# Attention with decay and a mixture of experts: q, k and v of a chunk laid out as four separate arrays

## The chip, the core and the metric

The kernel runs on one core of a Trainium2 chip. Its engines are TensorE (PE in the profile, with its weight loads as PEld), VectorE (DVE), ScalarE (ACT), GpSimd (POOL) and SyncE (SP), which here issues nearly all plain transfers; 16 DMA engines move the data between HBM and the core's SBUF. The metric is the device time of one execution in microseconds, as the median of several runs.

## What is computed

The inputs are q, k and v of shape (4, 8, 768, 64) (batch, heads, positions, head size) and a mixture of 8 experts, all in float32. The reference, cut to its core:

```python
for t in range(S):                                   # retention: attention with a decay per head
    state = gamma * state + einsum('bhd,bhe->bhde', k[:, :, t], v[:, :, t])
    y[:, :, t] = scale * einsum('bhd,bhde->bhe', q[:, :, t], state)
x = y.transpose(0, 2, 1, 3).reshape(B * S, H * D)    # 3072 tokens of 512
logits = x @ w_gate                                  # 8 experts, the best one takes the token
for e in range(E):
    xe = x[expert_idx == e]
    out[expert_idx == e] = gate_w * (maximum(xe @ w1[e], 0) @ w2[e])
```

## The kernel before

The 3072 tokens are cut into 24 chunks of 128 positions (`NCH`), six for each batch. For each chunk there are four blocks of 128 rows (SBUF partitions) and 512 floats: q transposed, k transposed, v and k, index 0 to 3 in that order. The host lays them out in one array `qkv` of shape (24, 128, 4, 512), so that one row of a chunk, all four blocks of it, is 8 KB in one piece in HBM.

The loop over chunks works on pairs, n = 0 to 11. For each chunk there are scores from q and k (`scores`, line 256, then a causal mask on DVE, line 259), the state's update from scaled v and k (`scale`, line 240, mostly on POOL, and `update`, line 271), the output from the scores and from the carried state (`output`, line 303, and `carry`, line 290), transposes to token rows (`rows`, line 322) and the gate's logits (`logits`, line 351, copied to LT by ACT at line 354, and turned back by PE as lp at line 363). The gating gives each token its expert and slot, and POOL scatters the token rows by indirect DMA (line 753) into `x_sorted` in HBM, where each expert has a region.

While that goes on, four loads of 1 MiB bring the weights of expert 0 (`fetch`, line 130, into tiles called raw: 128 rows of four pieces of 512 floats), and ACT and POOL or DVE split them into a high and a low part (lines 138 and 139).

The order on every engine is written out by hand; there is no planner. All of SP's transfers go through its one queue, in the order in which they are issued. `load(g)` (line 227) brings chunk g. Chunks 0 to 4 are brought as two halves, blocks 0 and 1 and then blocks 2 and 3 (512 KiB each), the other 19 whole (1 MiB). Four buffers of the pool `ld` and eleven of the pool `w` hold the chunks, so that SP issues the loads of chunks 0 to 14 at the start with no wait for a buffer, and those of chunks 15 to 23 as buffers come free. Two of the weight loads stand behind chunks 7 and 10 in the queue, the other two among the later chunks.

The last load, chunk 23, is followed on SP's queue by `start_rows` (line 453), which writes padding rows from the constants `cs` behind the rows of expert 0 in `x_sorted`, and by `fetch_early`, which waits for these rows and for the scatters of the first 18 chunks and brings the first 320 rows of expert 0 (line 148, tile xg). In the last pair, `turn_early` transposes them on DVE (line 768, xt), ACT casts them to the high part (line 775, xh), and PE uses xh in `early_pieces` (line 808, ph), the first work of the experts, which fills PE while the last gating is done. After that come the remaining rows of expert 0 and the other seven experts, ordered by their number of tokens, with two products each in three terms of high and low parts.

Of the kernel before, what the change touches and what calls it, by code (L numbers as in the profile page):

```python
# [18 lines left out]
E, DM, F = 8, 512, 1024  # L19
N = B * S  # L20
P = 128
# [3 lines left out]
NCH = B * CPB  # L25
# [75 lines left out]
def retention_moe(ctx, tc, qkv, w1, w2, cst, gdec, out):  # L101
    nc = tc.nc
# [101 lines left out]
    with ExitStack() as actx:  # L204
# [12 lines left out]
        qs, vss, Sbs, xTs, lgs, Ys, xrows = {}, {}, {}, {}, {}, {}, {}  # L217
# [4 lines left out]
        def load(g, part=slice(0, 4)):  # L222
            if g not in qs:
                early = AHEAD <= g < FIRST or g in MID
                qs[g] = (wp.tile([P, 4, DM], F32, name="qkv_w", tag="w", bufs=11) if early else
                         ld.tile([P, 4, DM], F32, name="qkv_t", tag="ld"))
            nc.sync.dma_start(out=qs[g][:, part], in_=qkv[g][:, part])

        def turned(g, i):
            return qs[g][:, i].rearrange("a (p t) -> a p t", p=NP)  # L230
# [259 lines left out]
        halves = (slice(0, 2), slice(2, 4))  # L490
        nc.vector.memset(wgs, 0.0)
        load(0, halves[0])
        gs = buf[0:2, 4 * NP * C:4 * NP * C + P + NP * C]
        nc.scalar.dma_start(out=gs, in_=gdec)
        nc.scalar.dma_start(out=cs[:, 0:NFIRST], in_=cst[:, 0:NFIRST])
        load(0, halves[1])
        for part in halves:
            load(1, part)
# [233 lines left out]
    natural = {0: (sidxs[0], metas[0]), E1: (sidxs[E1], metas[E1])}  # L732
# [484 lines left out]
```

## Time and profile before

| | |
|---|---|
| median of 3 runs | 395.36 us (394.53 to 395.36) |
| the profiled execution | 395.4 us |
| its span, first to last instruction | 393.5 us |
| PE busy | 385.6 us, 98% of the span |
| granted TensorE clock | 0.998 of full speed |
| DMA packets | 42332, 81.53 MB, 207 GB/s over the span |

The span leaves out what lies around the program's instructions, here 1.9 us. All stretches below are counted in microseconds from the span's start. PE's busy time says that it had an instruction in hand, not that it ran at its peak. In a stretch, the DMA share is the time that packets started in it took, over the time of 16 engines; it can pass 1.00, for the packets of one engine overlap somewhat.

### The profile page before, as it was taken

Reading aid. Unit: us, or ns where it says so; the run is one execution under the profiler, and the core shown is the slowest. Engines: PE = TensorE matmul, PEld = TensorE weight load, DVE = VectorE, ACT = ScalarE, POOL = GpSimd, SP = SyncE. Lnnn points to the kernel's source line nnn. Section 1 sums busy time; section 2 is a strip of 40 time slices with the busy share of each in tenths; the row PEclk is TensorE's granted clock in tenths of the full one; section 3 lists DMA queues with packets and bytes.
Section 4 is the critical chain, followed back from the end, with each engine's and each line's share of the span. In section 5 each row is a group of like instructions: output and inputs, shape, how many; then the busy total and the mean of one; then the engine's idle time right before and its main releaser. Section 6 shows DMA issues by size and latency. Waiting matters only on the chain.

```text
span 393.5 us, 8303 instructions
## 1 busy us (share of the span) xinstructions
PE 385.6 (98%) x3275; PEld 359.1 (91%) x3275; DVE 242.1 (62%) x467; ACT 141.3 (36%) x248; POOL 184.5 (47%) x175
## 2 busy tenths in 40 slices
PE   8999999999999899999999999999999999999994
PEld 4888888888999789999999999999999999999984
DVE  2567658966635796773874577386737658675310
ACT  2224344353311553532442354054335416423200
POOL 1656877784250427100682077038407813840743
PEclk9999999999999999999999999999999999999999
DMA  7999999983149759637472665564554636430111
GB/s 270 420 420 421 414 423 421 419 326 70 53 181 229 271 189 295 217 104 195 142 246 57 160 234 172 99 217 149 181 144 161 234 82 236 154 129 0 48 55 48
DMA packets 42332, 81.53 MB, mean 207 GB/s; under 512 B 4460, under 2 KB 18160, under 8 KB 39860
## 3 DMA queue, kind: packets, MB, share of 16 engines
q1 hardware_dynamic: 36768, 67.46, 50.7%
q0 software_dynamic: 5376, 13.49, 9.2%
q8 instruction: 26, 0.43, 0.4%
q14 instruction: 14, 0.11, 0.1%
q10 hardware_dynamic: 148, 0.04, 0.0%
HBM read 65.90 MB, written 15.68 MB: 207 GB/s over the span
## 4 chain that ended last, share of the span: by engine, by line
PE 94%; DVE 3%; issue 1%; ACT 1%; POOL 0%; POOLq 0%; DVEq 0%; ACTq 0%
PE ph L1050 31%; PE py L1078 27%; PE sp L256 5%; PE Y L303 5%; PE ph L808 4%; PE acc L827 4%; PE py L1076 3%; PE tr L322 3%; PE Y L290 3%; PE U L271 2%; PE L L351 2%; PE py L907 1%; PE py L968 1%; PE warm L507 1%; PE hn L951 1%
## 5 line engine op out<-in xcount | busy, mean ns | idle before, releaser
L753 POOL DMA_INDIRECT out<-Z,sidx x90 | 103.3, 1147 | 139.8 <-DVE Z L934 114.5
L139 DVE TENSOR_TENSOR wlo<-raw,whi 128x1024 fp32r<-128x1024 f32 (+1 forms) x57 | 68.4, 1205 | 14.3 <-ACT whi L138 13.9
L138 ACT CAST whi<-raw 128x1024 fp32r<-128x1024 f32 (+1 forms) x72 | 67.0, 950 | 8.2 <-DMA raw<-w 8.2
L1078 PE MATMUL py<-hh,whi 128*128 128x452 f32 (+5 forms) x192 | 66.9, 349 | 0.0
L1078 PE MATMUL py<-hl,whi 128*128 128x452 f32 (+5 forms) x192 | 66.9, 348 | 0.0
L1078 PE MATMUL py<-hh,wlo 128*128 128x452 f32 (+5 forms) x192 | 66.8, 348 | 0.0
L1055 ACT ACTIVATE hh<-ph 128x452 fp32r<-128x452 f32 (+6 forms) x56 | 28.3, 507 | 81.6 <-PE ph L1050 81.6
L1056 DVE SCALAR_TENSOR_TENSOR hl<-ph,hh 128x452 fp32r<-128x452 f32 (+6 forms) x56 | 32.1, 574 | 29.5 <-ACT hh L1055 29.0
L1050 PE MATMUL ph<-xh,wlo 128*128 128x452 f32 (+6 forms) x224 | 50.1, 345 | 0.0
L1050 PE MATMUL ph<-xh,whi 128*128 128x452 f32 (+6 forms) x224 | 50.1, 345 | 0.0
L1050 PE MATMUL ph<-xl,whi 128*128 128x452 f32 (+6 forms) x224 | 50.0, 345 | 0.0
L1050 PEld LDWEIGHTS ph<-xh,whi 128*128 128x128 f32 x224 | 40.8, 188 | 0.9
L1050 PEld LDWEIGHTS ph<-xh,wlo 128*128 128x128 f32 x224 | 40.8, 188 | 0.8
L1050 PEld LDWEIGHTS ph<-xl,whi 128*128 128x128 f32 x224 | 40.7, 188 | 0.7
L1078 PEld LDWEIGHTS py<-hl,whi 128*128 128x128 f32 x192 | 36.0, 188 | 0.8
L1078 PEld LDWEIGHTS py<-hh,wlo 128*128 128x128 f32 x192 | 36.1, 188 | 0.7
L1078 PEld LDWEIGHTS py<-hh,whi 128*128 128x128 f32 x192 | 36.1, 188 | 0.7
L775 ACT CAST xh<-buf 128x512 fp32r<-128x512 f32 (+7 forms) x26 | 14.3, 555 | 58.1 <-DVE buf L768 58.1
L259 DVE TENSOR_TENSOR Sb<-sp,cs 128x512 f32<-128x512 f32 x48 | 29.9, 681 | 2.7 <-PE sp L256 2.6
L753 POOL DMA_INDIRECT x_sorted<-xrow,KEY x24 | 24.2, 1008 | 15.1 <-DVE lp L391 7.3
L929 DVE STREAM_TRANSPOSE Z<-py 128x416 f32<-128x416 f32 (+3 forms) x24 | 15.0, 627 | 24.5 <-PE py L1078 24.4
L782 DVE TENSOR_TENSOR xl<-buf,xh 128x512 fp32r<-128x512 f32 (+7 forms) x26 | 18.1, 695 | 15.8 <-ACT xh L775 15.8
(172 smaller groups left out, 543.3 us busy)
## 6 DMA issues: line engine op xcount, KB each, us to landing
raw<-w SPq DMA_DIRECT2D x32, 1024.0 KB, 5.2
qkv_w<-qkv SPq DMA_DIRECT2D x12, 1024.0 KB, 18.5
qkv_t<-qkv SPq DMA_DIRECT2D x7, 1024.0 KB, 15.6
qkv_t<-qkv SPq DMA_DIRECT2D x8, 512.0 KB, 6.2
buf<-x_sorted SPq DMA_DIRECT2D x12, 211.2 KB, 3.7
x_sorted<-cs SPq DMA_DIRECT2D x6, 260.0 KB, 6.8
buf<-x_sorted SPq DMA_DIRECT2D x8, 195.0 KB, 3.6
out<-Z,sidx POOLq DMA_INDIRECT x90
```

The costliest lines, as they stand in the source:

```text
L138: nc.scalar.copy(out=hi[:, h], in_=raw[:, h])
L139: engine.tensor_tensor(out=lo[:, h], in0=raw[:, h], in1=hi[:, h].bitcast(F32), op=ALU.subtract)
L256: nc.tensor.matmul(out=sps[r][:, p, :], lhsT=kt[half[r], p, :], rhs=q[half[r], p, :], start=True, stop=True)
L259: nc.vector.tensor_tensor(out=Sb[:, r], in0=sps[r], in1=causal.unsqueeze(1).broadcast_to([P, NP, C]), op=ALU.mult)
L303: nc.tensor.matmul(out=at(Y, g, half[o], r, m), lhsT=vp[:, p, half[r]], rhs=Sb[:, r, p, :], start=False, stop=True, skip_group_check=True)
L753: sc = tc.nc.gpsimd.indirect_dma_start(out=dst, out_offset=bass.IndirectOffsetOnAxis(ap=index, axis=0), in_=rows, in_offset=None, bounds_c ...
L782: engine.tensor_tensor(out=xl[:, :, sl], in0=xt[:, :, t0:t0 + w], in1=xh[:, :, sl].bitcast(F32), op=ALU.subtract)
L808: nc.tensor.matmul(out=phs[f], lhsT=a[:, n % KD, fo:fo + P], rhs=h[:, n % KD, :], start=(n == 0), stop=(n == 11))
L1050: nc.tensor.matmul(out=ph[:, :cap], lhsT=wparts[e, f // 4][a][:, kd, fo:fo + P], rhs=x[:, kd, :cap], start=(n == 0), stop=(n == 3 * KD - 1))
L1055: nc.scalar.activation(out=hh[:, :cap], in_=ph[:, :cap], func=AF.Relu)
L1056: nc.vector.scalar_tensor_tensor(out=hl[:, :cap], in0=ph[:, :cap], scalar=0.0, in1=hh[:, :cap].bitcast(F32), op0=ALU.max, op1=ALU.subtract)
L1078: nc.tensor.matmul(out=py[:, :cap], lhsT=a[:, f % 4, k * P:(k + 1) * P], rhs=x[:, :cap], **se)
```

## The change

The host lays out the four blocks of a chunk one behind the other: `qkv` has the shape (24, 4, 128, 512), and a row of one block, 512 floats or 2 KB, is the longest piece that lies together for one partition. The load names the same elements in the same order of partitions, so the tiles in SBUF and all that reads them are as before; only the source's access pattern is another.

```diff
-            nc.sync.dma_start(out=qs[g][:, part], in_=qkv[g][:, part])
+            nc.sync.dma_start(out=qs[g][:, part], in_=qkv[g, part].rearrange("i p d -> p i d"))
...
-        "qkv": np.stack([transposed(q), transposed(k), natural(v), natural(k)], axis=3).reshape(NCH, P, 4, DM),
+        "qkv": np.stack([transposed(q), transposed(k), natural(v), natural(k)], axis=2).reshape(NCH, 4, P, DM),
```

A whole chunk was 128 pieces of 8 KB and is 512 pieces of 2 KB; a half was 128 pieces of 4 KB and is 256 of 2 KB. The host's layout is no part of the time.

## Rows read from the trace of the kernel before

**Rows 1.** The page: PE's busy time, and the DMA rate in 40 slices

```profile
PE 385.6 (98%) x3275; PEld 359.1 (91%) x3275; DVE 242.1 (62%) x467; ACT 141.3 (36%) x248; POOL 184.5 (47%) x175
...
GB/s 270 420 420 421 414 423 421 419 326 70 53 181 229 271 189 295 217 104 195 142 246 57 160 234 172 99 217 149 181 144 161 234 82 236 154 129 0 48 55 48
```

**Rows 2.** Windows: length, each engine's busy time and instructions, clock, DMA share, GB/s

```profile
97.00:128.00 31.00, 31.00 (x233) 30.11 (x230) 16.55 (x71) 7.39 (x20) 9.30 (x10) 1.00 0.53 149
128.00:393.00 265.00, 259.33 (x1400) 250.04 (x1398) 162.48 (x244) 97.92 (x142) 113.02 (x97) 1.00 0.50 157
```

**Rows 3.** DMA issues of the chunks: count, size of each, median us to landing

```profile
qkv_w<-qkv SPq DMA_DIRECT2D x12, 1024.0 KB, 18.5
qkv_t<-qkv SPq DMA_DIRECT2D x7, 1024.0 KB, 15.6
qkv_t<-qkv SPq DMA_DIRECT2D x8, 512.0 KB, 6.2
...
qkv_w<-qkv SPq DMA_DIRECT2D x2, 512.0 KB, 10.8
```

**Rows 4.** Windows, columns as in rows 2: stretches of 8, 2, 2, 4, 2 KB

```profile
57.00:62.00 5.00, 5.00 (x112) 4.44 (x112) 3.92 (x13) 1.35 (x5) 0.88 (x2) 1.00 1.02 429
24.00:26.00 2.00, 2.00 (x34) 1.36 (x25) 1.64 (x3) 0.81 (x2) 0.76 (x1) 1.00 1.09 428
34.00:36.00 2.00, 2.00 (x47) 1.81 (x43) 0.95 (x7) 0.24 (x1) 1.81 (x2) 1.00 1.02 393
...
10.00:13.00 3.00, 3.00 (x66) 2.66 (x64) 1.24 (x3) 0.37 (x1) 1.79 (x2) 1.00 1.03 422
126.00:132.00 6.00, 6.00 (x33) 5.22 (x32) 3.25 (x8) 3.27 (x5) 3.51 (x3) 1.00 1.05 407
```

**Rows 5.** DMA queues, packets, MB, share of 16 engines: 57:61, then 34.5:35.7 us

```profile
q1 hardware_dynamic: 231, 1.70, 100.7%
...
q1 hardware_dynamic: 214, 0.47, 102.4%
```

**Rows 6.** Timeline of SP's queue, 64 to 92 us: start, length, issue

```profile
64.44 6.82 SPq L227 DMA_DIRECT2D qkv_t<-qkv  x3
83.48 0.36 SPq L453 DMA_DIRECT2D x_sorted<-cs  x1
89.37 1.85 SPq L148 DMA_DIRECT2D xg<-x_sorted  x4
```

**Rows 7.** Landing of chunk 23 (issued 70.22), of start_rows; SP's wait for scatters

```profile
DMA to landing us min/median/max: 15.9/15.9/15.9
...
DMA to landing us min/median/max: 5.4/5.4/5.4
...
SPq L148 <- DMA x_sorted<-xrow,KEY: 5.4, 1, 5.4
```

**Rows 8.** Timeline, 94 to 98 us: the fetched rows on DVE, ACT and PE

```profile
94.73 1.63 DVE L768 STREAM_TRANSPOSE xt<-xg 128x512 f32<-128x512 f32 x3 [0.72 <-DMA xg<-x_sorted]
...
95.48 1.52 ACT L775 CAST xh<-xt 128x512 fp32r<-128x512 f32 x3 [0.98 <-DVE xt L768]
...
97.06 0.59 PEld L808 LDWEIGHTS ph<-xh,whi 128*128 128x128 f32 x4 [0.17 <-ACT xh L775]
```

**Rows 9.** Timelines near 19 and 39 us; landing of the weight load of 19.0

```profile
18.76 1.04 POOL L240 TENSOR_TENSOR vs<-qkv_w,cs 128x512 f32<-128x512 f32 x1 [1.92 <-DMA qkv_w<-qkv]
...
20.61 0.60 PEld L271 LDWEIGHTS U<-vs,qkv_w 128*64 128x64 f32 x16
...
DMA to landing us min/median/max: 19.4/19.4/19.4
...
38.12 1.14 ACT L138 CAST whi<-raw 128x512 fp32r<-128x512 f32 x2
39.89 0.37 ACT L354 COPY LT<-L 128x256 f32<-128x256 f32 x1 [0.64 <-PE L L351]
...
40.53 0.25 PEld L363 LDWEIGHTS lp<-cs,LT 128*128 128x128 f32 x2
```

## The prediction

> **What bounds the kernel now.** I read the page first: PE is counted busy for 98% of the span, and the DMA rate stands at 414 to 423 GB/s in the slices from 10 to 79 us, then falls [rows 1]. So there are two limits side by side in the first quarter (attention, which reads q, k and v): PE on its work, and the DMA engines on theirs. The windows by stage then show that behind 97 us PE has next to no idle time: 31.00 of 31 us, and 259.33 of 265 us, of which the rest is the tail after its last matmul [rows 2]. What makes PE late at 97 us is therefore paid in full at the end, and the question is only whether the loads make it late there or earlier.
>
> **What the change does to a load.** Nothing is computed differently and no instruction is added: 29 load issues on SP stay 29, of 19 x 1 MiB and 10 x 512 KiB [rows 3]. A whole chunk now comes in packets of 2 KB in place of 8 KB, so 512 packets in place of 128; a half chunk (two of the four arrays, so 4 KB in a row before) also comes in packets of 2 KB, 256 in place of 128. SP's cost of an issue I leave at nothing: its issues are hidden under a queue that is many microseconds deep (chunk 23 lands 15.9 us after its issue [rows 7]); without that cover it would be some tenths each.
>
> **The price of a smaller packet.** The trace has packets of all three sizes, because the weight loads (raw, 512 floats in a row) already come in 2 KB. With 8 KB packets alone the engines move 429 GB/s (57 to 62 us), with 4 KB packets 422 (10 to 13 us). Stretches that are mostly 2 KB packets give 393 (34 to 36 us) and 428 (24 to 26 us), both short, with packets of 8 KB at their edges, which are counted at their start; the one long stretch without 8 KB packets, 126 to 132 us, of 2 KB packets and some slightly larger writes, gives 407 [rows 4]. A second reading is free of these edges: bytes over the time that the packets themselves took. From 57 to 61 us that is 1.70 MB in 1.007 x 16 x 4 = 64.4 engine-us, 26.4 GB/s an engine; from 34.5 to 35.7 us it is 0.47 MB in 1.024 x 16 x 1.2 = 19.7 engine-us, 23.9 GB/s [rows 5]. That is 10% less, and an upper bound, for packets of one engine overlap somewhat (shares over 100%), and 2 KB ones can overlap more.
>
> I take 400 GB/s for 2 KB packets, between 393 and 407, and 429 and 422 for 8 KB and 4 KB. The 19 whole chunks are 19.92 MB: 49.8 us in place of 46.4, +3.4 us. The ten halves are 5.24 MB: 13.1 in place of 12.4, +0.7 us. Rounded, the sum is **+4.0 us** of DMA time up to the last chunk. Lower bound, at 407: (48.9 - 46.4) + (12.9 - 12.4) = +3.0; below that only if the 428 of 24 to 26 us is the true rate, which makes nothing of it. Upper bound, at 10% for whole chunks and half of that for halves: 4.6 + 0.6 = +5.2.
>
> The Trainium skill, "DMA: Bandwidth & Descriptors", section "Why small descriptors are slow (HBM only)", gives a fixed cost of some 3 cycles for each packet, beside one cycle for 32 bytes. By an estimate from that, four packets of 64 + 3 cycles stand against one of 256 + 3, 3.5% more (2.3% for halves): 46.4 x 0.035 + 12.4 x 0.023 = +1.9 us instead of +4.0. The rows ask for about twice that, and I go by the rows.
>
> **Whether the lateness adds up.** A late load is only passed on if the engines have no idle time in which to catch up. They have none from about 10 to 79 us: the slices hold one rate [rows 1], and the windows in them have packets in flight for over 100% of the time [rows 4]. The queue always holds several loads, because SP issues them as buffers come free, far ahead: 18.5 us is the median to landing of the 12 whole ones in the wide pool [rows 3]. So each chunk is late by the sum of all before it: some 0.8 us at chunk 4 or 5, about 1.8 us at the second weight load, nearly 4 us at chunk 23.
>
> **Where PE first feels it.** Early, at three near misses:
> - Chunk 4: POOL's scale waited 1.92 us for it and ended at 19.80; PE's update needs it at 20.61 [rows 9]. With 0.7 us (four chunks in halves and this one, 0.07 a half) it ends at 20.5: still in time.
> - The second weight load, issued at 19.0, lands after 19.4 us, at 38.4; the second of the two casts at 38.12 needs it, and behind them on ACT stands the copy of LT at 39.89, which PE waits for at 40.53 [rows 9]. Late by five chunks in halves (0.7) and six whole ones (1.0), so 1.7 us, it pushes the cast to 40.2 to 40.8 and LT's end to about 41.3: PE loses some 0.7 us here.
> - Later chunks have more room than they lose; PE, being 0.7 us later itself, gains as much room.
>
> These are no part of the sum, for PE's next meeting with the loads takes them in:
>
> **Where it is paid.** Behind load 23 on SP's queue stands the fill of padding rows in x_sorted (start_rows, issued at 83.48), and behind that the fetch of the first sorted rows (fetch_early). Chunk 23 was issued at 70.2 and landed 15.9 later, at 86.1; the fill landed after 5.4, at 88.9 [rows 6, 7]. SP waited 5.4 us from 83.84 for the last scatter of rows, to 89.24, and issued the fetch at 89.37 [rows 6, 7]. So the fill is only 0.4 us behind the gate. The rows fetched reached DVE's transposes at 94.73 (DVE had waited 0.72 us for them), ACT's casts to xh end at 95.48 + 1.52 = 97.00, and PE's first matmul on xh is at 97.06, after 0.17 us of waiting for ACT [rows 8]. That chain is tight from end to end. With chunk 23 late by 4.0, the fill goes behind it and lands at 92.9, the fetch leaves at 93.0, xh ends at 100.6, and PE, which would have been there at 97.8 after its early loss, waits for it. PE's loss at this point: 4.0 - 0.4 = **+3.6 us**, in place of the early 0.7 and not on top of it. The scatters that form the old gate share the engines with the loads; with 2 KB packets opposite theirs they get a larger share and do not become later than the fill.
>
> Behind 97 us PE has no idle time that could shrink [rows 2], and every later fetch depends on what PE and DVE compute, so it all moves together. The profiled execution took 395.4 us (span 393.5), the same as the median of the three runs, 395.36. **Forecast: 395.4 + 3.6 = 399.0 us.**
>
> **The rivals.**
> - *No cost at all*: 2 KB packets run at the rate of 8 KB ones, as the 428 of 24 to 26 us has it [rows 4], and the change does only what it says to the layout. Then chunk 23 lands at 86.1 as before and the time is 395.4, or 395.2 if the row scatters, which alternate with smaller packets, land up to 0.4 us earlier, down to the fill's landing. It decides as long as the lateness at chunk 23 stays under 0.4 us. Against it: 393 and 407 in the other two stretches. The Trainium skill, same page, "Rules for kernel authors", asks for 128 partitions and 1 MiB per DMA for full bandwidth and names no packet size; by that rule, which the whole chunks meet before and after, this rival is what happens. 0.13.
> - *Half the cost*: the mean of the two short stretches, 410 GB/s, is right. Then 19.92 MB take 48.6 us (+2.1) and the halves 12.8 (+0.4), 2.5 late, 2.1 paid: 397.5. For it: those stretches are the ones in this stage. The estimate from the skill's page above ends near here, at 395.4 + 1.9 - 0.4 = 396.9. 0.14.
> - *More than the sum*: packet time counts in full, 5.2 us late, 4.8 paid, 400.2; chunk 5 and chunk 15 then also reach PE's score matmuls late. Against it: the engines overlapped packets in every stretch. 0.07.
> - *Faster*: it would need a stretch in which four 2 KB reads beat one of 8 KB by more than 0.2%; no row shows one. What the smaller packets let through sooner (the scatters) frees at most the 0.4 us above. 0.04.
>
> **How the numbers follow.** The forecast has 0.62, about 398.0 to 399.9 (lateness of 3.0 to 4.9). Under 0.2% (0.8 us), about what a measurement of this kernel can tell from no change, lie the rival without cost and a little of the half-cost one. Slower: 0.62 + 0.14 + 0.07 - 0.01 = 0.82; same 0.14; faster 0.04. The range would leave out more than 2 in 10 if it stopped above the no-cost rival (0.13 + 0.04 below, and some 0.05 above 400.3), so it goes down to 395.3, which takes in the larger part of that rival, and up to 400.3, which takes in most of the high case.
>
> **What would show it.** In the new profile: packets under 8 KB nearly all; 395 to 405 GB/s in the slices from 10 to 80 us in place of 420; the stretch at that rate lasting some 4 us longer; chunk 23's landing near 90 and the fill's near 93; the fetch of xg near 93; PE's wait for xh before its first ph matmul grown from 0.17 to about 3 us, and a wait before lp near 41 us for LT. Behind that, each stage as long as before. I am wrong if the rate stays at 420 (no cost), if the rate falls but SP's fill and fetch do not move (the engines caught up somewhere), or if PE's total of waits before 90 us grows by more than the one at xh.

## The result, and the profile after

The kernel after the change takes 397.4 us (median of 20 runs, 395.43 to 399.95), the one before 394.7 in the same comparison (20 runs, 394.44 to 395.46). The ratio is 1.0069, interval 1.0049 to 1.0089: slower by 0.7%. The forecast was 399.0, in a range from 395.3 to 400.3. The profiled execution took 399.18 us, with a span of 397.4 us beside 393.5 before, so it is 3.9 us longer.

The 20 runs lie in two groups, ten from 395.4 to 396.8 and ten from 398.0 to 400.0. The mean granted clock is 0.996 to 0.999 in the lower group and 0.992 to 0.996 in the upper. No run took the median of 397.4, which is halfway between the groups. The profiled execution belongs to the upper one. No profile of the lower group was taken.

**The load rate.** From the page of the kernel after, PE's busy time and the DMA rate in 40 slices (against [rows 1]):

```profile
PE 386.7 (97%) x3275; PEld 359.8 (91%) x3275; DVE 241.8 (61%) x467; ACT 141.3 (36%) x248; POOL 184.6 (46%) x175
...
GB/s 298 400 405 405 406 408 407 407 358 74 0 189 166 361 115 302 223 167 173 155 179 94 193 167 231 71 197 191 161 169 137 247 76 225 168 133 0 48 54 48
```

The slices from 10 to 79 us stand at 400 to 408 GB/s in place of 414 to 423, and the ninth holds 358 in place of 326, because more is left to move. PE's busy time grew by only 1.1 us: the rest of the 3.9 us is idle time. PE's waits from 5 to 110 us are those of the kernel before (two of 0.2 and 0.3 us) and one more:

```profile
PE ph L808 <- ACT xh L775: 2.8, 1, 2.8
```

Windows of the kernel after, in the columns of [rows 2]; the first two are stretches of [rows 4], and the last two are what lies behind the first matmul on xh:

```profile
10.00:13.00 3.00, 3.00 (x62) 2.83 (x60) 1.24 (x3) 0.37 (x1) 2.58 (x3) 1.00 1.04 395
...
57.00:62.00 5.00, 5.00 (x108) 4.03 (x103) 4.05 (x11) 1.29 (x5) 1.22 (x2) 1.00 1.06 410
99.45:130.45 31.00, 31.00 (x220) 29.64 (x221) 14.96 (x68) 7.35 (x20) 8.29 (x9) 0.94 0.48 129
130.45:397.00 266.55, 260.80 (x1410) 251.48 (x1408) 163.36 (x246) 97.80 (x142) 114.05 (x98) 1.00 0.50 158
```

Pure chunk loads now run at 410 GB/s where they ran at 429 (57 to 62 us; E2 and E1 below have 405 and 428). Behind the first ph PE is again busy without a gap, 31.00 of 31 us, yet it gets through 220 matmuls in place of 233, at a mean clock of 0.94. Finer windows of the kernel after show where:

```profile
99.45:100.40 0.95, 0.95 (x6) 0.95 (x7) 0.95 (x3) 0.92 (x2) 0.41 (x1) 1.00 0.00 0
100.41:103.82 3.41, 3.41 (x20) 2.25 (x19) 2.23 (x13) 1.17 (x3) 0.00 (x0) 0.50 0.00 0
```

For 3.41 us TensorE is granted 0.50, that is 1.2 GHz in place of 2.4. Ahead of ph PE had stood idle for 2.8 us.

**The gate** is what SP waits for before it issues the fetch of the first sorted rows. The timeline of SP's queue after, 62 to 96 us, and SP's longest wait in that stretch (against [rows 6, 7]):

```profile
63.94 11.19 SPq L227 DMA_DIRECT2D qkv_t<-qkv  x3
82.76 0.38 SPq L453 DMA_DIRECT2D x_sorted<-cs  x1
90.77 1.85 SPq L148 DMA_DIRECT2D xg<-x_sorted  x4
```

```profile
SPq L148 <- DMA x_sorted<-cs: 7.5, 1, 7.5
```

What SP waits for ahead of the fetch is now the fill (x_sorted<-cs); before it was the last scatter of rows. By the semaphore records chunk 23 lands at 89.87 (86.09 before) and the fill at 90.63 (88.86 before). The last scatter, which was the gate before at 89.24, lands at 89.23. The fetch leaves at 90.77, 1.40 later than before.

SP's issues of the loads, which the prediction left at nothing, grew too: the three in the first line take 11.19 us in place of 6.82 with the waits between them [rows 6], that of chunk 23 alone 5.37 us in place of 1.04. At the gate this held nothing up: the fill was issued at 82.76, sooner than before.

The fetched rows on DVE, ACT and PE, from the timelines of the kernel after (against [rows 8]):

```profile
97.14 1.63 DVE L768 STREAM_TRANSPOSE xt<-xg 128x512 f32<-128x512 f32 x3 [3.63 <-DMA xg<-x_sorted]
...
97.89 1.52 ACT L775 CAST xh<-xt 128x512 fp32r<-128x512 f32 x3 [3.90 <-DVE xt L768]
...
99.45 0.59 PEld L808 LDWEIGHTS ph<-xh,whi 128*128 128x128 f32 x4 [3.06 <-ACT xh L775]
```

PE begins ph at 99.45, 2.39 us later than before. From there to the end of the span are 297.95 us, in place of 296.44: another 1.5, which the stretch at half clock explains. 2.4 + 1.5 = 3.9. The chain of work that ended last, in order of time (start, length, what), shows the path from the fetch to ph:

```profile
69.28 16.81 DMA qkv_t<-qkv
...
87.27 3.71 POOL wlo L139 x3
...
92.17 4.89 DMA xg<-x_sorted
...
97.14 0.72 DVE xt L768
...
97.89 1.52 ACT xh L775 x3
...
99.45 1.20 PE ph L808 x6
```

Its first two lines are not the path: the view puts the fetch down to the third of POOL's splits (wlo), which ended at 90.97, while the fetch's first issue was under way. In the kernel before the same split ended at 89.95, behind that issue (89.37 to 89.71), so the fetch does not wait for it. What ended SP's wait is the fill.

A piece of the path is the last quarter of the fetch: 4.89 us from its issue at 92.17 to its landing at 97.06. Before, the last quarter took 3.89, from 90.76 to 94.65. The DMA rate from 90.8 to 97.2 us, in 40 slices of 0.16 us, shows the last part of it as a trickle of a few packets, no slice above 16 GB/s from 95.3 us on:

```profile
GB/s 0 0 0 0 0 3 101 98 120 286 302 244 299 296 244 221 185 150 176 176 192 208 208 304 156 111 68 42 16 0 6 10 10 10 6 16 0 0 0 0
```

**Early.** The copy of LT near 39 us is not late, and PE's loads for lp follow at 40.02 without a wait (against [rows 9]; timelines of ACT and PEld after):

```profile
38.48 0.62 ACT L138 CAST whi<-raw 128x512 fp32r<-128x512 f32 x1 [0.25 <-issue]
39.38 0.38 ACT L354 COPY LT<-L 128x256 f32<-128x256 f32 x1 [0.29 <-PE L L351]
```

```profile
40.02 0.25 PEld L363 LDWEIGHTS lp<-cs,LT 128*128 128x128 f32 x2
```

### The profile page after: what moved, and what is told of

The parts are those of the page before. It is cut to its first block, busy times and chain, and to the rows that moved or that the text cites. A ratio compares the mean times of both kernels' runs of the same rounds, so it can differ in the third digit from the quotient of the medians.

```text
span 397.4 us, 8303 instructions
## 1 busy us (share of the span) xinstructions
PE 386.7 (97%) x3275; PEld 359.8 (91%) x3275; DVE 241.8 (61%) x467; ACT 141.3 (36%) x248; POOL 184.6 (46%) x175
## 4 chain that ended last, share of the span: by engine, by line
PE 88%; DMA 5%; DVE 1%; POOL 1%; ACT 1%; issue 1%; SPq 0%; POOLq 0%; DVEq 0%; ACTq 0%
PE ph L1050 31%; PE py L1078 27%; DMA qkv_t<-qkv 4%; PE sp L256 4%; PE ph L808 4%; PE acc L827 4%; PE Y L303 3%; PE py L1076 3%; PE tr L322 2%; PE Y L290 2%; PE U L271 2%; PE py L907 1%; PE py L968 1%; PE L L351 1%; DMA xg<-x_sorted 1%
## 5 line engine op out<-in xcount | busy, mean ns | idle before, releaser
L929 DVE STREAM_TRANSPOSE Z<-py 128x416 f32<-128x416 f32 (+3 forms) x24 | 15.0, 626 | 24.9 <-PE py L1078 24.9
## 6 DMA issues: line engine op xcount, KB each, us to landing
qkv_w<-qkv SPq DMA_DIRECT2D x12, 1024.0 KB, 13.2
qkv_t<-qkv SPq DMA_DIRECT2D x7, 1024.0 KB, 13.4
```

## The experiments

The theory: smaller packets make the loads later; the lateness is paid at one place, where PE waits for xh; and the idle time there costs some clock besides. The rivals: that the cost is in the queue order on SP (the fill behind load 23), that it comes once with any packet under 8 KB, or that it is spread over many small waits. E1 to E4 were timed beside a kernel before at 395.23 us (median of 14 runs, 394.46 to 395.56). In E5 to E12 the kernel before itself took 404 to 413 us (two single runs of 765 and 1486 us apart), so those are compared with that alone, and their traces with each other.

**E1, the kernel before once more** (no edit).

> The kernel before, unchanged, for a second trace. If the landings belong to the kernel: chunk 23 lands at 86.1 +- 0.5 us, the fill of x_sorted at 88.9, PE waits under 0.5 us for xh, the clock holds its upper level behind 97 us. PE's first score matmul and the clock's rise (6.3 us in the first trace, 4.8 in the changed kernel's) may lie anywhere between 4.8 and 6.3: if they are early here, the changed kernel's start, 0.6 us earlier, is no gain of the change. Rival: they are at 6.3 again, and the smaller first packets bring that gain.

It took 395.39 us. Chunk 23 landed at 86.55, the fetch left at 89.60, ph began at 97.14 after 0.17 us of waiting, and no stretch at half clock followed. PE's first weight loads on xh:

```profile
97.14 0.59 PEld L808 LDWEIGHTS ph<-xh,whi 128*128 128x128 f32 x4 [0.17 <-ACT xh L775]
```

So the two traces of the kernel before agree.

**E2, the kernel after once more** (no edit).

> The changed kernel, unchanged. Theory: DMA at 400 to 410 GB/s from 5 to 85 us, chunk 23 at 89.5 to 90, the fill at about 90.6, PE waits 2 to 3 us for xh; where a stretch of half clock follows that wait the run takes about 399, where none does about 396 to 397. Rival: the two groups of times come from the loads themselves (chunk 23 at 86 to 87 in the fast ones).

398.57 us (395.45 to 399.16), ratio 1.007, interval 1.0046 to 1.0094. Its timeline of PE's weight loads, and the window behind:

```profile
99.33 0.59 PEld L808 LDWEIGHTS ph<-xh,whi 128*128 128x128 f32 x4 [3.20 <-ACT xh L775]
```

```profile
100.30:103.60 3.30, 3.30 (x20) 2.13 (x19) 2.22 (x13) 1.08 (x3) 0.00 (x0) 0.50 0.00 0
```

The fetch left at 90.56, and ph waited 3.20 us. The same stretch of 3.41 us at 0.50 follows, from 100.28. The trickle at the end of the fetch is there too: the last quarter was issued at 91.96 and landed at 96.93. So what differs in the trace after does not come from one execution; but both profiled executions of this kernel (399.18 and 399.16 us) are of the upper group.

**E3, the fill sent by POOL** in place of SP, so that it does not stand behind load 23:

```diff
-            sent = nc.sync.dma_start(out=x_rows[bass.ds(start_at[0], P)], in_=cs[:, 0:ROW])
+            nc.vector.tensor_scalar(out=pad0, in0=full, scalar1=k_("pos")[:, 0:1], scalar2=0.0,
+                                    op0=ALU.add, op1=ALU.add)
+            sent = nc.gpsimd.indirect_dma_start(
+                out=x_rows, out_offset=bass.IndirectOffsetOnAxis(ap=pad0, axis=0),
+                in_=cs[:, 0:ROW], in_offset=None, bounds_check=x_rows.shape[0] - 1, oob_is_err=False)
```

> The changed layout, with the fill of padding rows sent through POOL's queue, so that it no longer stands behind load 23 in SP's. Theory (the fill behind chunk 23 is the gate): the gate falls back to the last row scatter at about 89.2 or to the fill at under 89.5, the fetch of xg leaves about 1.3 us earlier, PE's wait for xh shrinks from 2.8 to about 1.5 us, and the time is 395.5 to 396.5. Rival (the scatters, or one slow DMA engine, are the gate): nothing moves, 397.4. Rival (chunk 22 or 23 themselves stop PE): 397.4 or more.

The gate did not move: the fetch left at 90.93. SP's wait, and the first ph, in this kernel:

```profile
SPq L148 <- DMA x_sorted<-cs,pad: 8.2, 1, 8.2
```

```profile
98.52 0.59 PEld L813 LDWEIGHTS ph<-xh,whi 128*128 128x128 f32 x4 [1.64 <-ACT xh L780]
```

The fill, issued on another queue at 84.71, still landed only at 90.85, though it no longer stood behind chunk 23, which landed at 91.17. So the order on SP's queue alone does not set the gate; what fits is what the DMA engines have left to move, on whichever queue. (Over the first 80 us this execution moved 388 GB/s in place of 392, so it was 0.32 MB or 0.8 us behind the first trace after. That could hide a gain of 0.8 us, but not all of the 1.3 that I expected.) That part of my theory fell. The run is faster than E2 all the same, 396.2 us (396.06 to 396.77), ratio 1.0032, interval 1.002 to 1.0044: the fetch had no trickle (its last quarter landed at 96.08), PE's weight loads waited 1.64 us and not 3, and no stretch at half clock followed. Why this fetch has no trickle, in the layout of the kernel after, is open.

**E4, ten matmuls without use on PE ahead of the first ph**, so that PE does not stand idle while xh is late:

```diff
+        gap = bank(3, "gap", (P, 512))
+        for i in range(10):
+            nc.tensor.matmul(out=gap, lhsT=ones, rhs=ones.unsqueeze(1).broadcast_to([P, 4, P]),
+                             start=True, stop=True)
```

> The changed layout, with ten idle bf16 matmuls (2.1 us at full clock) on PE between the last output and the first ph. Theory (PE's idle 2.8 us before ph is followed by some 3.4 us at half clock): no such stretch, the upper group of times (398 to 400) is gone, the median is 395.5 to 396.8 although the matmuls add work. Rival (the half clock comes of itself): both groups stay and the median is 397.4 or higher. Rival (PE's wait is elsewhere): 2.1 us more, 399.5.

PE in the timeline of this kernel, and the windows behind it:

```profile
95.32 1.97 PE L303 MATMUL Y<-Sb,vs 128*64 128x128 f32 x32
97.22 2.33 PE L641 MATMUL gap<-ones 128*128 128x512 bf16 x10
99.20 0.94 PE L812 MATMUL ph<-xh,whi 128*128 128x320 f32 x4
```

```profile
96.50:99.30 2.80, 2.80 (x27) 1.57 (x22) 2.80 (x7) 2.44 (x5) 1.28 (x1) 1.00 0.01 3
100.30:103.60 3.30, 3.30 (x29) 2.72 (x28) 1.53 (x10) 2.11 (x5) 0.00 (x0) 1.00 0.00 0
```

ph begins only 0.15 us before that of E2, yet the span is 395.7 in place of 397.3, and the window of 3.3 us holds 29 matmuls in place of 20, at 1.00 in place of 0.50. So the half clock follows PE's idle time, and costs 1.4 to 1.5 us. The median missed what I expected (395.5 to 396.8): 397.86 (397.14 to 398.82), ratio 1.0073, interval 1.006 to 1.0086. No run lies at 395.5. That would follow if the filler runs to about 99.2 also where xh comes sooner, but only one of these runs was profiled.

**E5 to E8, parts of the layout, and a smaller packet.** E5 has chunks 0 to 4 in the new layout and the rest in the old one; E6 the reverse; E8 chunks 5 to 14 alone; E7 has all chunks in packets of 1 KB, eight half arrays in place of four.

```diff
-            nc.sync.dma_start(out=qs[g][:, part], in_=qkv[g, part].rearrange("i p d -> p i d"))
+            if g <= AHEAD:
+                nc.sync.dma_start(out=qs[g][:, part], in_=qkv[g, part].rearrange("i p d -> p i d"))
+            else:
+                nc.sync.dma_start(out=qs[g][:, part], in_=qkv8[g][:, part])
```

(E5; E6 has g > AHEAD in the condition, E8 AHEAD < g < FIRST; qkv8 is the layout of before.) E7, against the kernel before:

```diff
-            nc.sync.dma_start(out=qs[g][:, part], in_=qkv[g][:, part])
+            lo, hi = 2 * part.start, 2 * part.stop
+            nc.sync.dma_start(out=qs[g].rearrange("p i (s d) -> p (i s) d", s=2)[:, lo:hi],
+                              in_=qkv[g, lo:hi].rearrange("i p d -> p i d"))
```

> Chunks 0 to 4 (the ten half loads) in 2 KB packets, chunks 5 to 23 as before in 8 KB. Theory (the smaller packets give the start a lead: 3.0 MB moved by 10 us in place of 2.7, and cost only behind it): 3.0 MB by 10 us, then 420 GB/s, chunk 23 at about 85.5, no wait for xh above 0.3 us, time 394.3 to 395.4. Rival (halves cost 0.7 us like my forecast had it): 2.7 MB by 10 us, chunk 23 at 86.8, 395.4 to 396.

> Chunks 5 to 23 in 2 KB packets, the halves as before. Theory: 2.7 MB by 10 us, 405 GB/s from 15 to 80 us, so some 0.7 us later than the changed kernel everywhere behind 10 us; chunk 23 at about 90.4, the fetch of xg at about 91.4, PE waits 3 to 3.7 us for xh and some 3.4 us of half clock follow in most runs: 398 to 400, the median above the changed kernel's. Rival (the start's lead is worth nothing at the gate): the same as the changed kernel, 397.4 to 398.6.

> All chunks in packets of 1 KB. Theory (a fixed cost for each packet, about 2.5 us for the 24 extra packets of each of 19 chunks on each engine, so 5.4 ns a packet): 32 more packets a chunk are 0.17 us, 19 chunks 3.3 us and the halves 0.9: 385 to 390 GB/s, chunk 23 at 93 to 94, the fetch of xg at about 95, PE waits 6 to 7 us for xh and more where chunks come late, 401 to 404. Rival (a threshold below 2 KB): the rate falls far more, under 350 GB/s, and the time is over 408. Rival (the order of the queues at the end, not the packet): 397 to 399 as before.

> Only chunks 5 to 14 in 2 KB packets, loaded between 14 and 50 us; chunks 0 to 4 and 15 to 23 as before. Theory (the lateness of a chunk is carried to the end, since the engines have no idle time): 10 x 0.13 = 1.3 us late from 50 us on, the fetch of xg at about 90.3 to 90.8, PE waits about 1 us for xh, 395.8 to 396.8. Rival (only the last loads count, earlier lateness is caught up): 395.2, no wait for xh.

The times tell nothing apart, and none of the four times that I expected could be tested: 407.74 (ratio 1.0004, interval 0.9964 to 1.0045), 407.3 (1.0023, 0.9982 to 1.0063), 408.49 (1.0012, 0.9961 to 1.0063) and 408.41 (1.002, 0.9979 to 1.0061). The rates do. Windows of E8, where chunks 5 to 14 come in 2 KB and the rest in 8 KB:

```profile
40.00:50.00 10.00, 8.81 (x142) 7.03 (x143) 5.38 (x10) 2.10 (x5) 9.05 (x11) 1.00 1.05 407
50.00:60.00 10.00, 9.91 (x155) 7.97 (x152) 4.76 (x12) 5.03 (x11) 6.84 (x6) 1.00 1.03 424
```

The rate steps from 407 to 424 GB/s where the layout changes back: the price lies on the packets while they move. (E8's profile is of its slowest execution, 413.17 us, but E6 and E5 show the same two rates: in the same two windows 407 and 408 with chunks in 2 KB, 416 and 424 with chunks in 8 KB.) From the windows 10 to 80 us of the kernels before, after and E7, in that order:

```profile
10.00:80.00 70.00, 69.48 (x1272) 59.33 (x1268) 49.71 (x116) 26.45 (x65) 48.52 (x52) 1.00 1.02 420
```

```profile
10.00:80.00 70.00, 69.42 (x1267) 59.42 (x1265) 48.99 (x116) 26.88 (x66) 48.86 (x52) 1.00 1.05 405
```

```profile
10.00:80.00 70.00, 66.84 (x1202) 56.20 (x1194) 43.78 (x101) 24.10 (x58) 46.79 (x48) 1.00 1.08 390
```

420, 405 and 390 GB/s for 8, 2 and 1 KB in the chunk loads: at 16 engines 8 KB take 312, 324 and 336 ns, so 12 ns more for three packets more, and 24 for seven. That is an estimate of 3.4 to 4 ns a packet, mixed with traffic that did not change. Between 8 KB and 1 KB no threshold shows.

In the time it was all hidden. E7's first ph, and the row of DVE ahead of it:

```profile
103.97 0.59 PEld L810 LDWEIGHTS ph<-xh,whi 128*128 128x128 f32 x4 [0.17 <-issue]
```

```profile
100.83 1.62 DVE L770 STREAM_TRANSPOSE xt<-xg 128x512 f32<-128x512 f32 x3
```

Chunk 23 landed at 92.49 and the fetch's last quarter at 100.35, but DVE began its transposes at 100.83 without waiting for them: it was itself late. PE had lost some 7 us by then, at other places. From 36 to 96 us it was busy for 55.32 of 60 us, in E1 for 59.41. Part of the gaps are waits for the copy of LT (2.7 us in three places), part are not put down to any wait. What makes them, in the kernel before too, these runs do not show. They show what a cover does: with PE 7 us later at xh, PE did not wait for loads 6 us later. In the time a cost below some 0.6% would not show, by the interval.

**E9 and E12, packets of 1 KB again, and E10 and E11, one more load in the old layout**. E10 is the kernel before with a megabyte more to move, which nobody waits for:

```diff
             nc.sync.dma_start(out=qs[g][:, part], in_=qkv[g][:, part])
+            if g == 18:
+                nc.sync.dma_start(out=spare, in_=qkv[0])
```

(spare is a place in HBM of a chunk's size. E11 is E10 again; E9 and E12 are E7 again.)

> All loads of chunks in packets of 1 KB, half the size of the changed kernel's, once more. Theory A (the loads' time of transfer decides, because PE waits for xh, which waits for the fetch of xg behind the padding rows): where PE reaches ph at about 96.5 us as in the kernel before, the loads run at about 388 GB/s, chunk 23 lands at 92 to 93 us, the fetch of xg is issued at 93.9 to 94.9, ph begins at 102 to 103.5 after a wait of PE for xh of 5 to 7 us, TensorE's clock stands at half level for 3 us or so behind that, and the run takes 400.5 to 403 us. Theory B (the cost is not in the loads' time but in the form of the write into SBUF, once for all packets under 8 KB): 397 to 399.5, as with 2 KB. Where the kernel before takes 404 us or more, as beside the earlier run of this kernel, PE is at ph only at 104 and A expects no wait for xh and no difference.

> The kernel before, its loads in packets of 8 KB, with one transfer more of 1 MB (chunk 0 copied to a spare place in HBM that nobody reads) on SP's queue right behind the load of chunk 18; nothing waits for it. Theory A (lateness of the loads alone, by whatever way, makes the cost): at 420 GB/s the megabyte takes 2.5 us, so chunk 23 lands at 88 to 89.5, the fetch of xg is issued at 91 to 92.3, PE waits for xh for 1.5 to 3.5 us, the clock stands at half level for about 3.4 us behind it if the wait is as long as in the changed kernel, and the run takes 397 to 400 us. Theory B (it takes short packets beside the scatters or in SBUF to make it slower): 394.5 to 395.7, as the kernel before.

> The kernel before with the transfer of 1 MB more behind the load of chunk 18, once more, now to be read where the kernel before takes about 395 us and PE is at ph at 97. Theory A (lateness of the loads alone makes the cost): chunk 23 lands at 87.3 to 89 us, the fetch of xg is issued at 91 to 92.3, PE waits for xh for 1.5 to 3.5 us, the clock stands at half level for about 3.4 us behind a wait of 3 us, and the run takes 396.5 to 399.5 us. Theory B (it takes short packets): 394.5 to 395.7. Where the kernel before takes 404 us or more, both expect no difference.

> All loads of chunks in packets of 1 KB, to be read where the kernel before takes about 395 us. Theory A (the cost follows the rate: 420, 405 and 388 GB/s for 8, 2 and 1 KB): chunk 23 lands at 92 to 93, the fetch of xg is issued at 93.9 to 94.9, ph begins at 102 to 103.5, the clock stands at half level for 3 us or so behind it, and the run takes 400.5 to 403 us. Theory B (once for all short packets): 397 to 399.5. Where the kernel before takes 404 us or more, A expects no difference.

E9 took 407.27 us (ratio 0.9978, interval 0.9936 to 1.0019), E10 407.17 (0.9999, 0.9963 to 1.0036), E11 408.45 (1.0025, 0.9984 to 1.0065), E12 407.94 (0.9974, 0.9935 to 1.0013, and one run of 765 us), with the kernel before at 407.98 and 409.44. In all four ph waits 0.17 us for nothing that is a load, at 103.8 to 106.7, and chunk 23 lands at 92.24, 87.29, 86.59 and 92.58 by the last semaphore record that the traces hold. In E10 and E11 that is within 0.8 us of E1, so the megabyte did not make the loads late there. The rates repeat: 390 GB/s for 1 KB, 420 and 419 for 8 KB. These runs bear out what the theory says where PE is late, and only that. Whether a megabyte more in 8 KB packets costs the same 3 to 4 us where the kernel before takes 395 stays open, so lateness alone, without short packets, was not separated.

## Why the prediction was right, and where its steps were not

- **The rate.** Right in kind: 395 to 405 GB/s were foreseen, 400 to 408 came. The size was taken too large, 400 against 429, 7% more time for a byte. The same stretch measured 410 against 429, 4.6%, and all traffic from 10 to 80 us 405 against 420, 3.7%. The first 80 us held 401 GB/s before and 392 after, a lag of 9 x 80 us = 0.72 MB, or 1.8 us at 405; the sum had +4.0 up to the last load. The term that was mis-sized is the price of a 2 KB packet; the lower of the two short stretches (393) and the packets' own time (10%) misled me. The one long stretch, 407, which I took as the lower bound, and the mean of the two short ones, 410, which I gave to a rival, were nearest. The Trainium skill, "DMA: Bandwidth & Descriptors", section "Why small descriptors are slow (HBM only)", gave an estimate of 3.5% and +1.9 us, which I set aside; the measured 3.7% and 1.8 us agree with it, though for chunk loads alone the 4.6% is above it. For 1 KB the same rule of the Trainium skill makes 8.1% by an estimate (8 x 35 against 259 cycles); E7 has 390 against 420, 7.7%, also with other traffic in it.
- **The start.** I summed 0.7 us of lateness over the halves. There was none: the first 10 us moved 272 GB/s before and 300 after, a lead of 0.28 MB. Before has a dip to 140 GB/s near 9 us that after does not have. The halves alone (E5) moved 283, with low stretches of their own, so what removes it is open. The repeats agree (273 in E1, 299 in E2). This lead is why LT near 39 us was in time and the early loss of 0.7 us of PE did not occur: the second weight load, which I had 1.7 us late there, landed at 38.41 in both kernels.
- **Chunk 23.** Foreseen at +4.0, measured +3.8 (E2 against E1: +3.1), but not for the reason given. Only 1.8 us of it, the 0.72 MB at the full rate, is bytes. All of these bytes are of loads: from 65 to 80 us the scatters moved 1.60 MB in both kernels, at 26.3 and 26.1% of the engines' time. What was left from 80 to 91 us in the kernel before (packets, MB, share):

```profile
q0 software_dynamic: 480, 1.60, 37.3%
q1 hardware_dynamic: 409, 1.10, 26.7%
```

  and in the kernel after:

```profile
q1 hardware_dynamic: 905, 1.76, 41.3%
q0 software_dynamic: 480, 1.60, 36.1%
```

  (q0 has the scatters, q1 the loads and the fill; the 1.10 MB hold 0.08 of the fetch, which had begun.) The scatters are the same and no later than before. The loads have some 0.7 MB more to go, and share the engines with the scatters: from 80 to 88 us after they moved 1.59 MB, 199 GB/s of 395. By an estimate from that, 0.72 MB take 3.6 us. The larger share that I had foreseen for the scatters came, but for 5 us alone (27.9% before and 38.9% after from 70 to 75 us), and was given back in the next 5 (24.9 and 13.4%).
- **The fill and the fetch: the step that failed.** The prediction kept the fill 2.8 us behind chunk 23 and so put it at 92.9 and the fetch at 93.0. It came at 90.63, 0.76 behind chunk 23, and the fetch at 90.77, +1.4 and not +3.6. The fill moved by 1.77 us (E2 against E1: 1.12), near the lag in bytes (1.8 and 1.6) and not that of the last load (3.8 and 3.1); 0.4 of it was hidden, as foreseen, by the scatter that was the gate before. E3 agrees with that: with the fill on another queue the fetch left at 90.93.
- **PE's wait for xh.** Foreseen near 3 us, measured 2.8 to 3.1, again from other parts: +1.4 for the gate, +1.0 for the trickle at the end of the fetch, and PE being there 0.5 us sooner (its weight loads stood ready at 96.39 in place of 96.89). E3 and E4, without the trickle, had the last quarter at 96.08 and 96.03. What makes the trickle is open, and so is whether the packet size does: E3 and E4 have the layout of the kernel after, and in E11, with chunks in 8 KB, the last quarter took 5.4 us and ends in such a trickle.
- **Behind it.** "Each stage as long as before" was wrong: the first 3.4 us ran at half clock, +1.5 us. That made the profiled span 3.9 us longer, where +3.6 was forecast from a wait alone. So the path was right, and that the number is near owes something to luck: the gate, forecast 2.2 us too late, was made up for by the trickle and the clock, 1.0 and 1.5, which were not forecast.
- **The median.** 399.0 holds for the upper group, not for the median of 397.4. The groups fit the two things that vary: a wait near 3 us with half clock behind it, and one near 1.6 without (E3: 396.2). The mean of the lower group, 396.1, is 1.4 above the kernel before, as much as the gate moved. That the lower runs of the kernel after are of that second kind was not seen in a profile. It is argued from this, from E3 and from their higher mean clock, and one run of E2 (397.3 us at a clock of 1.000) fits neither kind.

The rival with half the cost, 397.5 us, had the rate nearly right and lies on the median, but by a sum that has neither the trickle nor the clock. The rival without cost asked for less than 0.4 us of lateness at chunk 23; it was 3.8 there and 1.4 at the gate. E5 to E12 show how it could have come true: with PE some 7 us later at xh.

## What to carry to other kernels

Where the DMA engines have no idle time, price a packet size by a long stretch of pure traffic, and add up the lag in bytes; here the fill that made the gate moved by about that lag (1.8 us, in the repeat 1.1), and not by that of the last load (3.8 and 3.1), which shared the engines with the scatters at the end. Then look at what waits for the gate: a wait of about 3 us on PE cost 1.5 us more behind it in clock, and where PE came 7 us later for other reasons it did not wait for the loads at all. A change that loses 4% of a load rate is worth undoing only if such a gate stands behind it; here one does, and the rows of 8 KB are the faster layout by 0.7%.

## What was not expected of the hardware

- After 2.8 and 3.0 us in which no matmul ran (after, E2) the granted clock fell to 0.50, not at once but 0.95 us after PE had begun again, and stayed there for 3.41 us in both. After 1.4 us (E3), and with PE kept busy (E4), it did not fall.
- How two queues share the engines swung with the packet size of one: opposite loads of 2 KB in place of 8 KB the scatters' share of time from 70 to 75 us rose from 27.9% to 38.9% (E1 27.7, E2 41.6), and from 75 to 80 us it fell from 24.9% to 13.4% (E1 25.1, E2 10.7). They were served sooner, and no more of them.
- SP took longer to issue a load of as many bytes in smaller packets: 2.39 us in the median for the 14 issues into the pool `w`, in place of 0.50. The 12 whole chunks among them were issued 13.2 us ahead of their landing in place of 18.5.
- The kernel before, unchanged, took 394.4 to 395.6 us in some comparisons and 404 to 413 in others (E1 to E8 ran on one and the same chip), with matmuls as long as before (274 ns for Y in both E1 and E5) but with gaps between them. A comparison of 0.7% holds only beside the kernel before in the same comparison, and where that is at 407 this change cannot be seen.
